# Top-k attention with an ELU feed-forward: the nine transposes of a step issued together, and their copies moved ahead of a mask

## The chip, the cores and the metric

The kernel runs on one core of one Trainium2 chip. The metric is the device time of one execution in microseconds (us), lower is better. Engines are named as in the profile: PE is TensorE (PEld its weight loads), DVE is VectorE, ACT is ScalarE, POOL is GpSimd, SP is SyncE.

## What is computed

Attention over 8 batches, 8 heads, 576 positions and 64 elements a head, in which each query row keeps only its 32 largest scores, and then a feed-forward over the 4608 rows that come out (512 to 2048 to 512), with an ELU between. The two weights are float64, so the kernel reads them as pairs of 32-bit words and makes float32 of them on the chip.

```python
scores = scale * np.matmul(q, k.transpose(0, 1, 3, 2))
kth = np.partition(scores, -32, axis=-1)[..., -32:-31]
scores = np.where(scores >= kth, scores, -1e9)
attn = np.exp(scores - np.max(scores, axis=-1, keepdims=True))
attn = attn / (np.sum(attn, axis=-1, keepdims=True) + 1e-09)
out = np.matmul(attn, v)
# (B, H, S, D) -> x of (B*S, H*D)
h = x @ w_in
g = np.where(h > 0.0, h, np.exp(np.minimum(h, 0.0)) - 1.0)
y = g @ w_out
```

## The kernel before, in words

**Steps.** The work is cut into 144 steps: 8 batches of 18. A step is a tile of 128 queries of one batch and a pair of heads, so it has two "rows" of scores, each 128 partitions by 576 keys. Of each batch 64 queries are left over; for them a step takes four heads, so that 128 partitions are full. Steps come in groups of two query tiles that share one attention product (in batch 0, and for the left-over queries, of a single tile).

**The loop** (L702) works on four steps at once. In iteration n it does, in this order of issue:

- scores of step n+2 (`scores`, L331), into two PSUM tiles `wide[0]` and `wide[1]` of two banks each, evicted by ScalarE into the tile `sc` (L339);
- the attention product of a group that is complete (`attend`, L470): 10 matmuls, each recorded twice in the profile, so that a run on two tiles shows 20; its result is copied by L497;
- the selection of step n on VectorE in four passes (`select`, L373, L378, L385): the 32 largest of each row, eight at a time;
- the mask of step n-1, one row ahead of the second pass and the other ahead of the third (`mask`): GpSimd takes a difference (L406), ScalarE makes the mask (L407) and the exponential with its sum (L408), in place in `sc`;
- the transposes of step n-2 (`turn`, L444, each a matmul with the identity) and their copies to the tile `et` on ScalarE (L445);
- the normalisation of step n-1 on GpSimd (`normalise`, L418 to L423 for the reciprocal of the sum, L425 for the two rows).

A step's `sc` is 128 by 1152, that is nine chunks of 128 columns. `turn` is called for three parts of them: `main` (chunks 0 to 3, all in the first row), `rest` (chunk 4, whose second half is in the second row) and `other` (chunks 5 to 8, in the second row). `main` and `other` each take a buffer of `ps_t`, a PSUM pool of two buffers that `attend` uses too. `rest` takes 128 columns beside the scores in the second bank of `wide[1]`, so the next scores wait for its copy.

**What is fed between.** Once a block of one to three tiles has all its heads, its feed-forward is cut into pieces: `hidden` (L545, w_in; two evictions by L555 and L558, an exponential by L560, minus one by L564 or inside the closing addition, which runs on GpSimd, L515, or VectorE, L517) and `project` (L573, w_out; evicted by L582, stored by SyncE, L585). They share a PSUM pool of two buffers. `feed` is called four times an iteration and issues as many pieces as the steps left and the work left ask for. In an iteration the pieces of the third feed stand between `rest` and `other`, those of the fourth between `other` and the next scores.

**Order.** From step 8 on the instructions of PE, ACT, DVE and POOL stand exactly in the order in which the code issues them; each engine takes its own in that order. The first eight steps are ordered by a scheduler and, beside their attention, hold the conversion of the weights. SyncE's transfers are not ordered by hand.

**Buffers that matter here.** `sc` has five buffers, `et` two, `ps_t` two. The tile `kqT`, with keys and queries transposed, has five; from batch 1 on VectorE fills it (L285), in the same order as its selections.

Of the kernel before, what the change touches and what calls it, by code (L numbers as in the profile page):

```python
# [24 lines left out]
class Tile:  # L25
# [6 lines left out]
    def __init__(self, b, qt, rows, block, cols):  # L32
        self.b, self.qt, self.rem = b, qt, qt == 4
        self.rows = rows
        self.block = block
        self.cols = cols
        self.ql = cols.stop - cols.start
# [21 lines left out]
class Step:  # L59
# [7 lines left out]
    def __init__(self, t, hp, group, at):  # L67
        self.t, self.hp = t, hp
        self.group, self.at = group, at
        self.masked = self.normal = self.turned = False  # L70
        if t.rem:
            rows = [(4 * hp, 0), (4 * hp + 2, 0), (4 * hp + 3, 1), (4 * hp + 1, 1)]
            self.heads = [
                (h, i, slice(64 * (n % 2), 64 * (n % 2) + 64))
                for n, (h, i) in enumerate(rows)
            ]
        else:
            self.heads = [(2 * hp + i, i, slice(0, 128)) for i in range(2)]
# [3 lines left out]
def kernel(  # L82
# [13 lines left out]
    J = S // P  # L96
# [216 lines left out]
    def turn_qk(whole=False):  # L313
        while turning:
            if next(turning[0], turning) is turning:
                turning.pop(0)
            elif not whole:
                return
# [3 lines left out]
    def scores(u):  # L322

        u.sc = scpool.tile([P, 2, S], FP32, tag="sc", name="sc")
        q0 = (QUERIES if u.t.b == 0 else S) + u.t.qt * P
        for half in range(2):
            for h, i, rows in u.heads:
                kq = kqT[u.t.b, h // 2]
                part = slice(i * D, (i + 1) * D)
                k0 = (KEYS if i == 0 and u.t.b == 0 else 0) + half * HS  # L330
                nc.tensor.matmul(  # L331
                    wide[i][rows, half, 0:HS],
                    kq[part, q0 : q0 + u.t.ql],
                    kq[part, k0 : k0 + HS],
                    start=True,
                    stop=True,
                )
        for i in range(2):
            nc.scalar.activation(  # L339
                u.sc[:, i, :].rearrange("p (a s) -> p a s", a=2),  # L340
                wide[i][:, :, 0:HS], AF.Copy, scale=scale,
            )

    def select_row(u, i, decoding):
        if i == 0:
            u.first = small.tile([P, 2, 8], FP32, tag="m1", name="m1")
            u.last = small.tile([P, 2, 8], FP32, tag="m4", name="m4")
        sc = u.sc[:, i, :]
        m = u.first[:, i, :]
        nc.vector.max(m, sc)  # L350
        wk = wkpool.tile([P, S], FP32, tag=f"wk{i}", name="wk")
        cur = sc
        for r in range(TOP_K // 8 - 1):
            nc.vector.match_replace(wk[:], m, cur, TAKEN)
            cur = wk[:]
            if r < TOP_K // 8 - 2:
                m = small.tile([P, 8], FP32, tag=f"m{i}", name="m")[:]
            else:
                m = u.last[:, i, :]
            nc.vector.max(m, cur)  # L360
            if r > 0 and decoding:
                hook()
            if r != 1:
                yield
# [64 lines left out]
    def turn(u, chunks):  # L429

        if u.turned:
            return
        g = u.group
        if g.et is None:
            g.et = etpool.tile([P, 2 * J + 1, len(g.tiles), P], FP32, tag="et", name="et")
        if chunks.stop - chunks.start == 1:
            ps = wide[1][:, 1, HS : HS + P]
        else:
            ps = ps_t.tile([P, JP], FP32, tag="t", name="eps")
        sc = u.sc[:, :, :].rearrange("p i s -> p (i s)")  # L440
        n = chunks.stop - chunks.start
        for c in range(n):
            c0 = (chunks.start + c) * P
            nc.tensor.transpose(ps[:, c * P : (c + 1) * P], sc[:, c0 : c0 + P], ident[:])  # L444
        nc.scalar.copy(  # L445
            g.et[:, chunks, u.at, :],
            ps[:, 0 : n * P].rearrange("p (c q) -> p c q", c=n),
        )
        if chunks.stop == 2 * J + 1:
            u.turned = True  # L450
            if u.at == len(g.tiles) - 1:
                closing.append(g)

    def attend(g):
        t = g.tiles[0]
        ps = ps_t.tile([P, JP], FP32, tag="t", name="avps")
        n = P if t.rem else sum(x.ql for x in g.tiles)
        for k in range(2 if t.rem else 1):
            hp = 2 * g.hp + k if t.rem else g.hp
            vt = vT[t.b, hp]  # L460
            for c in range(J + 1):
                for i in range(2):
                    chunk = J if c == J else i * (J + 1) + c
                    w = g.et[:, chunk, :, :].rearrange("p a q -> p (a q)")
                    cols = slice(0, n)
                    if t.rem:
                        c0 = R * (k if i == 0 else 1 - k)
                        w = w[:, c0 : c0 + R]
                        cols = slice(k * R, (k + 1) * R)
                    nc.tensor.matmul(  # L470
                        ps[i * D : (i + 1) * D, cols],
                        vt[:, 2 * J + i if c == J else i * J + c, :],
                        w,
                        start=(c == 0),
                        stop=(c == J),
                    )
        if t.rem:
            finish(t.block, 2, slice(2 * g.hp, 2 * g.hp + 2), t.cols,
                   ps[:, 0:n].rearrange("p (a q) -> p a q", a=2))
            return  # L480
        c0 = 0
        tiles = list(g.tiles)
        while tiles:
            blk, lo, parts = tiles[0].block, tiles[0].cols.start, 0
            while tiles and tiles[0].block is blk:
                parts += 1
                hi = tiles.pop(0).cols.stop
            finish(blk, parts, g.hp, slice(lo, hi), ps[:, c0 : c0 + hi - lo])
            c0 += hi - lo
# [112 lines left out]
    for b in range(B):  # L602
# [28 lines left out]
        for qts in order:  # L631
# [3 lines left out]
            for qt in qts:  # L635
                n = len(steps)
# [60 lines left out]
    def step(n):  # L697
        return steps[n] if 0 <= n < NS else None

    closing = []  # L700
    main, rest, other = slice(0, J), slice(J, J + 1), slice(J + 1, 2 * J + 1)
    for n in range(NS + 3):  # L702
        for fn, args in todo.pop(n, []):
            fn(*args)
        ahead, cur, prev, done = step(n + 2), step(n), step(n - 1), step(n - 2)
        if n < tight:
            turn_qk(True)
            if n < 3:
                scores(ahead)
            if n > 1:  # L710
                scores(step(n + 3))
            for i in range(2):
                passes = select_row(cur, i, n < tight - 1)
                next(passes)
                if i == 0:
                    while closing:
                        attend(closing.pop(0))
                elif prev:
                    normalise(prev)
                    turn(prev, main)  # L720
                    turn(prev, rest)
                    turn(prev, other)
                feed(n, 0.25)
                next(passes)
                mask(cur, i, True)
                feed(n, 0.25)
            continue
        if n == tight:
            ctx.enter_context(tc.manual_schedule(engines=engines))
        passes = select(cur) if cur else iter(range(4))  # L730
        if ahead and n > tight:
            scores(ahead)
        while closing:
            attend(closing.pop(0))
        next(passes)
        feed(n, 0.25)
        if prev:
            mask(prev, 0)
        turn_qk()
        next(passes)  # L740
        feed(n, 0.25)
        if done:
            turn(done, main)
            turn(done, rest)
        if prev:
            mask(prev, 1)
        next(passes)
        feed(n, 0.25)
        if done:
            turn(done, other)  # L750
        next(passes)
        if prev:
            normalise(prev)
        feed(n, 0.25)
        turn_qk(True)
# [36 lines left out]
```

## Time and profile before

| what | value |
|---|---|
| runs, median (lowest to highest) | 1643.64 us (1641.84 to 1643.79) |
| profiled execution, its own time | 1642.57 us |
| its span, first to last instruction | 1640.8 us |
| mean granted TensorE clock over the span | 0.974 |
| ACT: COPY of L445, 128x512, mean of 288 | 571 ns |
| ACT: COPY of L445, 128x128, mean of 144 | 269 ns |
| ACT: L407 and L408, mean of 288 each | 782 and 776 ns |
| POOL: L425, mean of 288 | 750 ns |
| DVE: MAX8 of L385, mean of 816 | 752 ns |
| PE: L444 into `ps_t`, mean of 1152 | 279 ns |
| PE: L470, mean of 2080 | 330 ns |

Matmuls are pipelined, so the mean of one is longer than the distance from one start to the next; distances between starts tell what a matmul costs on TensorE. A wait in the profile is idle time of an engine just before an instruction, put down to what released it. Where PEld waits but PE does not, the wait was partly covered by matmuls still running.

### The profile page before, as it was taken

To read this page: it belongs to the slowest core of one execution; us is meant where nothing else is said; L and a number is where in the kernel's file an instruction comes from. 1 tells how busy PE (TensorE), PEld (TensorE's weight loads), DVE (VectorE), ACT (ScalarE), POOL (GpSimd) and SP (SyncE) were. 2 spreads that over 40 slices of the span, in tenths; PEclk is the share of its full clock that TensorE was granted. 3 is DMA by queue.
4 is the path that set the end of the run, shared out by engine and by line. 5 is a ranking of instruction groups with operands and counts; after the bars stand their busy time and mean duration, and the time that the engine had idled before them with its cause. 6 is when DMAs were issued, how large, how long until landed. Compare 5 with 4: busy or idle time off the path is not lost.

```text
span 1640.8 us, 25344 instructions
## 1 busy us (share of the span) xinstructions
PE 1581.7 (96%) x8276; PEld 1011.8 (62%) x8276; DVE 1453.4 (89%) x2981; ACT 1187.7 (72%) x2400; POOL 708.7 (43%) x1534
## 2 busy tenths in 40 slices
PE   4788999999999999999999999999999999999999
PEld 3566777666575757555566666655557575755564
DVE  6987999999999999999999699999999599998000
ACT  6887778778695867778678686868759595958521
POOL 4775445445353534445335353535435353534300
PEclk8579999999999999999999999999999999999999
DMA  7431221012100310012100211012100201000000
GB/s 226 151 128 25 50 40 26 7 22 45 42 1 7 59 42 8 7 22 44 36 14 15 43 30 28 1 28 44 36 14 0 43 1 35 1 13 2 7 13 14
DMA packets 188037, 56.18 MB, mean 34 GB/s; under 512 B 178177, under 2 KB 179201, under 8 KB 187905
## 3 DMA queue, kind: packets, MB, share of 16 engines
q1 hardware_dynamic: 186704, 54.26, 14.1%
q8 instruction: 66, 1.08, 0.3%
q14 instruction: 67, 0.54, 0.1%
q10 hardware_dynamic: 1200, 0.30, 0.1%
HBM read 45.09 MB, written 9.44 MB: 33 GB/s over the span
## 4 chain that ended last, share of the span: by engine, by line
PE 76%; ACT 12%; DVE 7%; POOL 3%; issue 1%; DMA 1%; SPq 0%; ACTq 0%; DVEq 0%; POOLq 0%
PE ops L573 29%; PE hps L545 23%; PE avps L470 10%; PE scps L331 7%; PE eps L444 6%; DVE wk L378 3%; DVE m L385 3%; ACT sc L408 2%; ACT et L445 2%; ACT sc L407 2%; DVE m L373 1%; ACT n L564 1%; ACT n L555 1%; ACT sc L339 1%; ACT n L560 1%
## 5 line engine op out<-in xcount | busy, mean ns | idle before, releaser
L385 DVE MAX8 m<-wk 128x8 f32<-128x576 f32 x816 | 577.9, 752 | 0.3 <-POOL den L406 0.3
L545 PE MATMUL hps<-xT,w_in 128*128 128x256 f32 (+2 forms) x2432 | 545.8, 374 | 0.0
L573 PE MATMUL ops<-w_out,gT 128*128 128x512 f32 x1152 | 523.6, 599 | 0.0
L545 PEld LDWEIGHTS hps<-xT,w_in 128*128 128x128 f32 x2432 | 406.0, 192 | 100.1 <-issue 26.3
L378 DVE MATCH_REPLACE8 wk<-m,wk 128x576 f32<-128x576 f32 x544 | 401.4, 748 | 0.0
L573 PEld LDWEIGHTS ops<-w_out,gT 128*128 128x128 f32 x1152 | 209.0, 190 | 233.9 <-issue 232.8
L418 POOL TENSOR_SCALAR dene<-den 128x2 f32<-128x2 f32 x144 | 32.9, 228 | 686.5 <-ACT sc L408 686.1
L408 ACT ACTIVATE sc<-sc,den 128x576 f32<-128x576 f32 x288 | 223.6, 776 | 65.5 <-POOL den L406 44.2
L407 ACT ACTIVATE sc<-sc,m 128x576 f32<-128x576 f32 x288 | 225.3, 782 | 10.8 <-DVE m L385 10.7
L470 PE MATMUL avps<-et,vT 128*64 128x256 f32 (+2 forms) x2080 | 207.2, 330 | 17.4 <-ACT et L445 17.2
L425 POOL TENSOR_SCALAR sc<-sc,rec 128x576 f32<-128x576 f32 x288 | 213.0, 750 | 15.0 <-POOL rec L423 0.2
L331 PE MATMUL scps<-kqT 64*128 64x288 f32 (+1 forms) x1280 | 206.0, 442 | 13.6 <-ACT kqT L307 9.1
L339 ACT ACTIVATE sc<-scps 128x576 f32<-128x576 f32 x288 | 171.8, 647 | 65.1 <-PE scps L331 65.1
L445 ACT COPY et<-eps 128x512 f32<-128x512 f32 x288 | 164.6, 571 | 73.4 <-PE eps L444 73.4
L378 DVE MATCH_REPLACE8 wk<-m,sc 128x576 f32<-128x576 f32 x272 | 200.6, 748 | 0.0
L373 DVE MAX8 m<-sc 128x8 f32<-128x576 f32 x272 | 191.6, 749 | 8.8 <-ACT sc L339 8.8
L444 PEld LDWEIGHTS eps<-ident,sc 128*128 128x128 f32 x1152 | 144.9, 144 | 87.2 <-issue 52.7
L444 PE MATMUL eps<-ident,sc 128*128 128x128 f32 x1152 | 177.1, 279 | 13.7 <-POOL sc L425 13.7
L470 PEld LDWEIGHTS avps<-et,vT 128*64 128x64 f32 x2080 | 128.5, 142 | 98.8 <-ACT et L445 31.7
L515 POOL TENSOR_TENSOR gT<-n,gT 128x512 f32<-128x512 f32 (+1 forms) x119 | 164.9, 1386 | 31.2 <-ACT n L564 31.1
L331 PEld LDWEIGHTS scps<-kqT 64*128 64x128 f32 (+1 forms) x1280 | 111.3, 182 | 89.5 <-issue 43.8
L555 ACT ACTIVATE n<-hps 128x512 f32<-128x512 f32 (+1 forms) x156 | 87.3, 559 | 56.8 <-PE hps L545 56.0
(53 smaller groups left out, 1089.6 us busy)
## 6 DMA issues: line engine op xcount, KB each, us to landing
raw<-in_moe_w_in_dram SPq DMA_DIRECT2D x16, 512.0 KB, 6.1
vT<-in_v_dram SPq DMA_DIRECT2D x64, 128.0 KB, 2.5
raw<-in_moe_w_out_dram SPq DMA_DIRECT2D x16, 512.0 KB, 3.6
out_dram<-osb SPq DMA_DIRECT2D x32, 256.0 KB, 2.1
kin<-in_k_dram SPq DMA_DIRECT2D x112, 72.0 KB, 2.5
qin<-in_q_dram SPq DMA_DIRECT2D x112, 72.0 KB, 2.6
kin<-in_k_dram SPq DMA_DIRECT2D x8, 128.0 KB, 4.5
vT<-in_v_dram SPq DMA_DIRECT2D x64, 16.0 KB, 2.2
```

The source lines that it names most:

```text
L331: nc.tensor.matmul(wide[i][rows, half, 0:HS], kq[part, q0 : q0 + u.t.ql], kq[part, k0 : k0 + HS], start=True, stop=True,)
L373: nc.vector.max(found[i], cur[i])
L378: nc.vector.match_replace(wk[i], found[i], cur[i], TAKEN)
L385: nc.vector.max(found[i], cur[i])
L407: nc.scalar.activation(sc, sc, AF.Prelu, scale=-1.0, bias=low, alpha=1.0 / STEEP)
L408: nc.scalar.activation(sc, sc, AF.Exp, scale=-STEEP, bias=gap, accum_out=u.den[:, i : i + 1])
L425: nc.gpsimd.tensor_scalar(u.sc[:, i, :], u.sc[:, i, :], rec[:, i : i + 1], 1.0, ALU.mult, ALU.mult)
L444: nc.tensor.transpose(ps[:, c * P : (c + 1) * P], sc[:, c0 : c0 + P], ident[:])
L445: nc.scalar.copy(g.et[:, chunks, u.at, :], ps[:, 0 : n * P].rearrange("p (c q) -> p c q", c=n),)
L470: nc.tensor.matmul(ps[i * D : (i + 1) * D, cols], vt[:, 2 * J + i if c == J else i * J + c, :], w, start=(c == 0), stop=(c == J),)
L545: nc.tensor.matmul(blk.h[:, f % bank, :], w_in[:, i, f * P : (f + 1) * P], blk.xT[:, i, 0:n_tok], start=(i == 0), stop=(i == NC - 1),)
L573: nc.tensor.matmul(blk.o[:], blk.gT[f // NG][:, f % NG, s * P : (s + 1) * P], w_out[:, f, :], start=(f == 0), stop=(f == NF - 1),)
```

## The change

The four transposes of `other` are issued right after those of `main`, and `rest` after both, all ahead of the second row's mask and of the third feed. On ScalarE the two large copies and the small one then stand in one row ahead of the second row's L407 and L408; before, the copy of `other` stood behind that mask and behind the evictions of the third feed's pieces. A counter of chunks that are still to be turned takes the place of the test for the last chunk, since `other` is no longer the last call. The first eight steps keep their order of calls.

```diff
@@ class Step
         self.masked = self.normal = self.turned = False
+        self.left = 9
@@ turn
-        if chunks.stop == 2 * J + 1:
+        u.left -= n
+        if u.left == 0:
             u.turned = True
             if u.at == len(g.tiles) - 1:
                 closing.append(g)
@@ the loop
         if done:
             turn(done, main)
+            turn(done, other)
             turn(done, rest)
         if prev:
             mask(prev, 1)
         next(passes)
         feed(n, 0.25)
-        if done:
-            turn(done, other)
         next(passes)
```

## The prediction

> **What bounds the kernel now.** First the page: busy shares and the slices.
>
> ```profile
> PE 1581.7 (96%) x8276; PEld 1011.8 (62%) x8276; DVE 1453.4 (89%) x2981; ACT 1187.7 (72%) x2400; POOL 708.7 (43%) x1534
> ...
> PE   4788999999999999999999999999999999999999
> ...
> DVE  6987999999999999999999699999999599998000
> ```
>
> TensorE and VectorE are both full from the fifth slice on, so busy time alone doesn't say which sets the pace. I settled it with the timeline, step by step: the lag between the end of a step's last MAX8 (L385) and the start of that step's transposes (L444) two iterations later. It shrinks from 25.3 us (step 9) to 7.1 us (step 25, 317 us): there TensorE catches up and VectorE sets the pace. Then it grows: 10.5 us at 340, 13 at 500 to 600, 18 at 715, 30 at 915. So VectorE runs ahead and **TensorE sets the pace from about 340 us to the end**. The waits view says how VectorE's lead ends: its L285 transposes are held by the scores matmuls, once 14.2 us (before 931 us), once 16.9 us (before 1310 us). From 800 to 930 us the steps repeat at 11.53 and 9.22 us by TensorE's own work.
>
> ```profile
> DVE kqT L285 <- PE scps L331: 32.3, 3, 16.9
> PEld avps L470 <- ACT et L445: 31.7, 40, 3.8
> ...
> PE avps L470 <- ACT et L445: 17.2, 21, 3.3
> ...
> PE eps L444 <- POOL sc L425: 13.7, 5, 4.3
> ```
>
> (Columns: total us, times, longest.) The second and third lines are the wait that the change touches: the attention matmuls wait for the copy of the last four transposes. The fourth is where a later mask would show: transposes that wait for normalised rows. The timeline of one such step:
>
> ```profile
> 1487.09 0.60 PE L444 MATMUL eps<-ident,sc 128*128 128x128 f32 x4
> ...
> 1487.52 0.27 PE L444 MATMUL scps<-ident,sc 128*128 128x128 f32 x1
> ...
> 1489.67 0.57 ACT L445 COPY et<-eps 128x512 f32<-128x512 f32 x1
> ...
> 1490.13 0.27 ACT L445 COPY et<-scps 128x128 f32<-128x128 f32 x1
> 1490.21 0.60 PE L444 MATMUL eps<-ident,sc 128*128 128x128 f32 x4
> ...
> 1490.29 0.79 ACT L407 ACTIVATE sc<-sc,m 128x576 f32<-128x576 f32 x1
> ...
> 1491.92 0.65 PE L470 MATMUL avps<-et,vT 128*64 128x256 f32 x2
> ...
> 1492.68 0.59 ACT L445 COPY et<-eps 128x512 f32<-128x512 f32 x1
> ...
> 1493.32 2.37 PE L470 MATMUL avps<-et,vT 128*64 128x256 f32 x18 [0.76 <-ACT et L445]
> ```
>
> The last copy stands behind the second row's mask (L407, L408) and a block's evictions; 18 of the 20 attention matmuls wait for it. From 1491.92 to the next matmul (L545 at 1495.62) is 3.70 us; unhindered runs take 2.31.
>
> **The change, part by part.**
>
> (a) *The last copy no longer stands behind the mask.* I took every run of L470 after 300 us from its first matmul to the next other matmul. 24 of 55 runs on two tiles take 2.31 us, so that is the work. The excess of the others that start after 340 us adds up to 21.6 us, and one run of the remainder tiles has 0.93: **22.5 us**, 14.6 of it before 900 us. In the changed order the copy is issued 0.46 us after the main one (two L445 copies follow each other at that distance: 1489.67, 1490.13), and all three end before the scores matmuls do. All 22.5 go. What is late next is the remaining copy's release of the scores bank, (d).
>
> (b) *The run at 325 us.* Scores wait 2.46 us and attention 2.28 us there, at the end of VectorE's stretch. The second wait goes, the first grows by 0.46: **+1.8**.
>
> (c) *The single transpose comes after the four.* At 379, 540, 560, 767 and 1147 us it waited 0.51 to 0.77 us after the main four, for row two (L425's second half, 0.73 us behind the first) and for the scores' eviction (L339) from its bank. The four need row two as well, but not the bank: about 0.3 each, **+1.5**.
>
> (d) *Scores wait longer for their bank.* The single transpose's copy frees the bank that the next scores write; it now ends 0.46 us later, and the scores start when they did, since TensorE's work between is the same. Six steps are short of it already (at 379, 502, 560, 595, 684, 745 us): the full 0.46, 2.8 us. Eleven have 0.34 to 0.45 us of slack where they need 0.51: 1.1 us together. **-3.9**.
>
> (e) *The second row's mask starts 0.46 us later.* Queued behind it on ScalarE are the evictions of the fed blocks, and then L339; GpSimd's normalisation (L418 to L425) waits for it, and so do the next step's transposes. Slack of L425's end before those transposes: 1.1 to 8.7 us in nearly all steps after 340 us, typically 1.72 in the 9.22 us steps (1.44 for row two). Evictions have at least 1.5 us before their banks are needed again. So most of it is hidden. Without cover are the short steps of 7.5 us (at 379, 540, 560, 767, 1147 us), with 0.05 to 0.09 of slack: five times 0.46, **-2.3**.
>
> (f) *What VectorE doesn't let through.* Between 340 and 660 us the lag is small. A step's transposes can't start sooner after VectorE than the chain mask, copies, mask, normalisation takes: 6.2 us to the first normalised row in step 39 (450 us), where the first mask starts at once, and 6.7 with the added copy; about 9 to 10 where a block's evictions stand between the masks (5.5 us between them in step 51 in place of 2.3). At step 41 that leaves 2.0 us to gain, at step 51 3.4, at step 53 3.8, at step 59 5.8. The gains and losses above add up to 9.4 by step 59 (663 us); walked through these ceilings 5.4 are left: **-4.0**. Past that the lag grows faster than the gains, and both holds of VectorE (14.2 and 16.9 us) end with TensorE's scores, so they move with it.
>
> (g) *TensorE's work itself.* Starts are 0.109 us apart within the four, across to the single one, and from either to the next matmul; only towards scores is a step longer, 0.202 after transposes, and 0.093 is added after L545 or L573 instead. Regrouping moves that from one place to another: **0**. VectorE and GpSimd keep their order of instructions; on SyncE one q load changes places with an output store (landing 2.6 and 2.1 us, steps ahead of their use): 0, and 2.6 if that cover were gone. No transpose waits on its two-buffer pool: the bank that attention used is freed by L497, ahead of the masks on ScalarE; only at 410 us do transposes follow attention directly, 0.3 at most.
>
> Sum: 22.5 + 1.8 + 1.5 - 3.9 - 2.3 - 4.0 = **15.6 us**. The profiled execution took 1642.57 us (span 1640.8); 1642.57 - 15.6 = **1627.0**. The median of the runs shown is 1643.64, 0.07% above that execution.
>
> Two pages speak against it. By the Trainium skill, "Perfetto Trace Analysis", Identifying the Most-Contended Engine, matmul busy time is a poor measure and weight loading's busy share is to be used: 62% here, so VectorE (89%) would be the bound, and the time would stay near 1642.6. The lag in this trace says otherwise after 340 us. "TensorE: Matmul & The Clock Gate", Part 4, gives about 275 ns for a transpose in a kernel and says that transposes don't count as activity for the clock; nine in a row would be 2.5 us by it, against 0.98 by the trace's 0.109 us, and the mask would be late by some 1.1 us, still less than the usual slack. The granted clock of so long a run no row shows.
>
> **The rivals.**
>
> *All of it gets through.* VectorE's ceilings in (f) don't bind, since ScalarE's waits move too: 19.6 us, 1623.0; without (d) and (e) as well, 25.8 and 1616.8. For it: ceilings rest on single steps. Against: lags of 9 to 13 us up to 600 us.
>
> *VectorE is the bound up to 900 us.* It is busy 200.00 of 200.00 us in each window from 300 to 900 us. Then only later waits count: 7.9 (a), less about 1 for (d) and (e): 6.9 us, 1635.7. Against: the lag grows by 20 us in that stretch.
>
> *The wait is only renamed.* ScalarE reaches the main copy up to 5.4 us after its transposes (step 25); were it so late everywhere, attention would wait as before: 1642.6. Against: typical 0.3 to 3.1 us.
>
> *Slower: the mask's delay exceeds the slack.* The place is L407 of row two, behind a copy that waits for four more transposes. If one wait held all three copies for all nine transposes it would be 0.9 us late, still inside. It decides from 1.44 us (the slack of the single transpose in 9.22 us steps); some 58 steps then lose 0.58 us per 0.01 us, so 15.6 us are eaten at 1.7. At 2.0 us: 32 lost, 1659. For it: every step passes there. Against: no row shows such a wait.
>
> **How the numbers follow.** Forecast (gain 9 to 21 us) 0.60; all through 0.14; VectorE's bound 0.13; renamed 0.06; slower 0.07. Range: 1618.5 takes in all-through with smaller losses, 1637.0 the VectorE case with (d) and (e) doubled; 0.85 or so lies inside. A measurement of this kernel can tell some 0.2% (3.3 us) from no change: faster 0.87, same 0.06, slower 0.07.
>
> **What would show it.** Right: the waits of L470 for L445 are gone, runs of L470 take 2.31 us; L331's waits for L445 have grown to a few us; the first mask-to-mask distance is 0.46 us longer; steps at 800 to 930 us still repeat at 9.22 and 11.53; VectorE's two holds at L285 are shorter or equal, and the stretch from 1530 us to the end is 1.5 us shorter. Wrong: L444 waits for L425 in the 9.22 us steps (the mask's delay matters), or L470's waits are gone and the step times are longer (the clock, or transposes waiting for buffers), or the lag at 600 us is below 7 us and stays there (VectorE's bound).

## The result, and the profile after

The changed kernel takes **1631.73 us** (median of 6 runs, 1630.5 to 1633.75) where the kernel before takes 1643.25 (6 runs, 1641.61 to 1644.53): a ratio of 0.9933, 95% interval [0.992, 0.9945], 11.5 us or 0.7% less. The forecast was 15.6 us less, 1627.0. The profiled execution took 1631.07 us, span 1629.3, mean granted TensorE clock 0.977 (before 0.974).

The code stands one line lower than before after line 70 and two lower after line 449: L331 is now L332, L406 to L408 are L407 to L409, L425 is L426, L444 and L445 are L445 and L446, L470 is L472.

First the page of the changed kernel: busy time of the engines, and the slices of PE and DVE.

```profile
PE 1573.0 (97%) x8276; PEld 1005.0 (62%) x8276; DVE 1451.7 (89%) x2981; ACT 1185.9 (73%) x2400; POOL 710.6 (44%) x1534
...
PE   4788999999999999999999999999999999999999
...
DVE  6988999999999999999999799999999699999000
```

Next to nothing is to be seen in these lines: shares within a point, the same full slices. The waits view (total us, times, longest) shows what happened. Of the kernel before, the scores' wait for the copies, which stands beside the lines shown ahead of the change:

```profile
PEld scps L331 <- ACT et L445: 4.7, 8, 2.2
...
PE scps L331 <- ACT et L445: 1.7, 1, 1.7
```

And of the changed kernel:

```profile
PEld eps L445 <- POOL sc L426: 29.5, 34, 3.7
...
DVE kqT L286 <- PE scps L332: 25.7, 3, 16.3
...
PEld scps L332 <- ACT et L446: 19.1, 25, 3.1
PE eps L445 <- POOL sc L426: 17.9, 12, 3.4
...
PE scps L332 <- ACT et L446: 8.8, 9, 2.7
...
PEld avps L472 <- ACT et L446: 5.1, 4, 3.7
PE avps L472 <- ACT et L446: 3.8, 2, 3.3
```

The attention's wait for the copies has gone from 31.7 to 5.1 us on PEld (17.2 to 3.8 on PE), and what is left of it lies ahead of 340 us. The scores' wait for the same copies, which before was 4.7 on PEld and 1.7 on PE, is now 19.1 and 8.8, and the transposes wait a little more for GpSimd. The wait was taken away at one place, and a good half of it came back at another. The timeline of the step that was shown before makes the first half plain:

```profile
1477.98 1.04 PE L445 MATMUL eps<-ident,sc 128*128 128x128 f32 x8
...
1478.85 0.27 PE L445 MATMUL scps<-ident,sc 128*128 128x128 f32 x1
...
1480.57 1.06 ACT L446 COPY et<-eps 128x512 f32<-128x512 f32 x2
...
1481.51 0.28 ACT L446 COPY et<-scps 128x128 f32<-128x128 f32 x1
...
1483.01 2.38 PE L472 MATMUL avps<-et,vT 128*64 128x256 f32 x20
```

Eight transposes and the single one follow each other, the copies stand in one row, and the attention product runs through in 2.31 us from its first matmul to the next other matmul (1485.32), where it took 3.70.

**A ledger.** To compare kernels I add up, from step 27 (340 us) to the end, what each kind of run on TensorE takes beyond its unhindered time: attention beyond 2.31 us, scores beyond 1.17 us (first matmul of the run to the first of the next; the steps of left-over queries go by their own least times), and the transposes' waits, ahead of the nine and between them. The sums are of figures that aren't rounded. Each line is of one profiled execution, the time beside it the median of the runs.

| us after 340 us | attention | scores | transposes | sum | time (median) |
|---|---|---|---|---|---|
| before | 22.6 | 3.1 | 3.6 | 29.4 | 1643.25 |
| after | 0.0 | 16.1 | 5.0 | 21.2 | 1631.73 |

29.4 - 21.2 = 8.2; by the trace, the lead of the changed kernel grows from 3.1 us at step 27 to 11.5 at the end, that is 8.4. The ledger accounts for the difference after 340 us. So the question is why the scores lost 13.0 us where the forecast had 3.9.

### The profile page after: what moved, and what is told of

The parts are those of the page before. It is cut to its first block, busy times and chain, and to the rows that moved or that the text cites. A ratio compares the mean times of both kernels' runs of the same rounds, so it can differ in the third digit from the quotient of the medians.

```text
span 1629.3 us, 25324 instructions
## 1 busy us (share of the span) xinstructions
PE 1573.0 (97%) x8276; PEld 1005.0 (62%) x8276; DVE 1451.7 (89%) x2981; ACT 1185.9 (73%) x2400; POOL 710.6 (44%) x1534
## 4 chain that ended last, share of the span: by engine, by line
PE 69%; DVE 15%; ACT 8%; POOL 5%; issue 2%; DMA 1%; SPq 0%; ACTq 0%; DVEq 0%; POOLq 0%
PE ops L575 26%; PE hps L547 21%; PE avps L472 8%; PE scps L332 7%; DVE wk L379 6%; PE eps L445 5%; DVE m L386 5%; DVE m L374 2%; ACT sc L409 2%; ACT et L446 2%; POOL sc L426 1%; ACT sc L408 1%; POOL rec L421 1%; DVE wk L355 1%; DVE m L361 1%
## 5 line engine op out<-in xcount | busy, mean ns | idle before, releaser
L386 DVE MAX8 m<-wk 128x8 f32<-128x576 f32 x816 | 685.3, 1015 | 1.1 <-POOL den L407 0.8
L379 DVE MATCH_REPLACE8 wk<-m,wk 128x576 f32<-128x576 f32 x544 | 472.4, 1010 | 0.0
L409 ACT ACTIVATE sc<-sc,den 128x576 f32<-128x576 f32 x288 | 224.0, 778 | 90.0 <-POOL den L407 69.3
L408 ACT ACTIVATE sc<-sc,m 128x576 f32<-128x576 f32 x288 | 227.1, 788 | 19.5 <-DVE m L386 19.4
L332 PE MATMUL scps<-kqT 64*128 64x288 f32 (+1 forms) x1280 | 215.8, 443 | 21.2 <-ACT kqT L308 9.3
L379 DVE MATCH_REPLACE8 wk<-m,sc 128x576 f32<-128x576 f32 x272 | 235.8, 1008 | 0.0
L374 DVE MAX8 m<-sc 128x8 f32<-128x576 f32 x272 | 227.0, 1009 | 6.1 <-ACT sc L340 6.1
L426 POOL TENSOR_SCALAR sc<-sc,rec 128x576 f32<-128x576 f32 x288 | 214.0, 754 | 14.9 <-POOL rec L424 0.2
L332 PEld LDWEIGHTS scps<-kqT 64*128 64x128 f32 (+1 forms) x1280 | 114.4, 182 | 123.6 <-issue 61.1
L472 PE MATMUL avps<-et,vT 128*64 128x256 f32 (+2 forms) x2080 | 186.1, 326 | 3.8 <-ACT et L446 3.8
L379 DVE MATCH_VALUE_LOAD wk<-m,wk 128x8 f32 x544 | 187.2, 344 | 0.0
L445 PEld LDWEIGHTS eps<-ident,sc 128*128 128x128 f32 x1152 | 136.6, 144 | 70.6 <-issue 33.1
L446 ACT COPY et<-eps 128x512 f32<-128x512 f32 x288 | 153.5, 582 | 34.6 <-PE eps L445 34.1
L445 PE MATMUL eps<-ident,sc 128*128 128x128 f32 x1152 | 158.3, 279 | 18.7 <-POOL sc L426 17.9
L517 POOL TENSOR_TENSOR gT<-n,gT 128x512 f32<-128x512 f32 (+1 forms) x119 | 165.3, 1389 | 17.9 <-ACT n L566 17.8
L472 PEld LDWEIGHTS avps<-et,vT 128*64 128x64 f32 x2080 | 118.9, 141 | 74.6 <-issue 24.8
```

The source lines that it names most:

```text
L332: nc.tensor.matmul(wide[i][rows, half, 0:HS], kq[part, q0 : q0 + u.t.ql], kq[part, k0 : k0 + HS], start=True, stop=True,)
L374: nc.vector.max(found[i], cur[i])
L379: nc.vector.match_replace(wk[i], found[i], cur[i], TAKEN)
L386: nc.vector.max(found[i], cur[i])
L408: nc.scalar.activation(sc, sc, AF.Prelu, scale=-1.0, bias=low, alpha=1.0 / STEEP)
L409: nc.scalar.activation(sc, sc, AF.Exp, scale=-STEEP, bias=gap, accum_out=u.den[:, i : i + 1])
```

## The experiments

Three theories stood at first. **A**: the copy of `other` ahead of `rest` and of the mask delays both by about 0.48 us, and the mask's delay returns through GpSimd's queue to ScalarE's next copies. **B**: VectorE's pace takes back what TensorE gains, as step (f) of the forecast had it. **C**: only the place of the `rest` copy counts, 0.48 us behind, which frees the scores' bank later.

What A means is best seen in one step of 9.22 us. The timeline before, and the same step after:

```profile
870.92 1.47 POOL L425 TENSOR_SCALAR sc<-sc,rec 128x576 f32<-128x576 f32 x2
...
873.38 0.60 PE L444 MATMUL eps<-ident,sc 128*128 128x128 f32 x4
...
873.59 0.19 POOL L406 TENSOR_TENSOR den<-m,m 128x1 f32<-128x1 f32 x1
...
873.81 0.78 ACT L408 ACTIVATE sc<-sc,den 128x576 f32<-128x576 f32 x1 [0.58 <-POOL den L406]
...
876.74 0.57 ACT L445 COPY et<-eps 128x512 f32<-128x512 f32 x1
...
877.20 0.27 ACT L445 COPY et<-scps 128x128 f32<-128x128 f32 x1
...
877.91 1.24 PE L331 MATMUL scps<-kqT 64*128 64x288 f32 x8
```

```profile
863.73 1.48 POOL L426 TENSOR_SCALAR sc<-sc,rec 128x576 f32<-128x576 f32 x2
...
865.70 1.04 PE L445 MATMUL eps<-ident,sc 128*128 128x128 f32 x8
...
866.43 0.19 POOL L407 TENSOR_TENSOR den<-m,m 128x1 f32<-128x1 f32 x1
...
866.65 0.78 ACT L409 ACTIVATE sc<-sc,den 128x576 f32<-128x576 f32 x1 [1.09 <-POOL den L407]
...
869.58 1.06 ACT L446 COPY et<-eps 128x512 f32<-128x512 f32 x2
...
870.23 1.86 PE L332 MATMUL scps<-kqT 64*128 64x288 f32 x8
...
870.52 0.28 ACT L446 COPY et<-scps 128x128 f32<-128x128 f32 x1
...
870.86 0.78 PEld L332 LDWEIGHTS scps<-kqT 64*128 64x128 f32 x6 [0.33 <-ACT et L446]
```

Measure from the step's first transpose (873.38 before, 865.70 after). The normalisation of two rows starts 2.46 us ahead of it before and 1.97 after: it is 0.49 later, since the second row's mask was. Behind it on GpSimd stand half of a block's addition (L515, now L517, 1.3 us) and then the mask difference of the next step: 0.21 us after the first transpose before, 0.73 after. ScalarE's exponential waits for that difference, 1.09 us in place of 0.58. So ScalarE's whole row is late, and the main copy starts 3.88 us after the transposes in place of 3.36. On top of that, the `rest` copy stands one more copy behind. It ends 5.10 us after the first transpose in place of 4.09: 1.01 later, of which 0.52 is this round trip and 0.49 the place in the row. The scores, which were ready at the same moment, take 1.86 us in place of 1.24.

**1. `rest` copied first, `other` still ahead of the mask.** This takes away the place in the row and leaves the mask's delay.

```diff
             turn(done, main)
-            turn(done, other)
             turn(done, rest)
+            turn(done, other)
         if prev:
             mask(prev, 1)
```

> Order main, rest, other, all ahead of the second row's mask: the scores' bank is freed 0.48 us sooner than in the changed kernel, the mask starts as late as there. Theory A (two delays, the bank's and the mask's; the mask's comes a second time through GpSimd, where the next mask's difference L406 stands behind the late normalisation): the scores' waits after 340 us fall from 16 to about 8 us, those of the normal steps (870, 954, 1038 us and so on, 0.62 to 0.65 each) to about 0.15, transposes still wait for the normalisation as in the changed kernel; 3 to 6 us faster than it, 1626 to 1629. Theory C (only the bank's release counts): scores' waits fall to the 3 us of the kernel before, 1620. Theory B (VectorE's pace doesn't let TensorE gain more): 1631 to 1632 as in the changed kernel, with a wait of the same size elsewhere.

Measured: 1625.77 us (1623.47 to 1626.37), ratio 0.9894 [0.9878, 0.9909]. The scores' excess falls from 16.1 to 8.6 us; the waits of 0.6 us in the repeating steps after 760 us shrink to 0.1, since the slack there covers one of the two delays and not both. It speaks against B, which left no room for a gain, and against C, since 5.5 us of the 13.0 stay although `rest` is again where it was.

**2. `other` copied right behind the mask, still ahead of the feed.**

```diff
             turn(done, main)
-            turn(done, other)
             turn(done, rest)
         if prev:
             mask(prev, 1)
+        if done:
+            turn(done, other)
         next(passes)
         feed(n, 0.25)
```

> The four transposes of other stand behind the second row's mask, but ahead of the third feed: the copy waits for the mask and no longer for the feed's evictions; neither the mask nor the bank is later than in the kernel before. Theory A: waits of scores and of the transposes as in the kernel before (3 us and its few), attention's waits not gone but about 10 of 22.5 us left, since the mask's 1.75 us still stand ahead of the copy (0.9 where nothing is fed, 0.4 to 0.5 in the odd steps): 1629 to 1632, much like the changed kernel by another road. Theory C: the same. Theory B: the same time too, but with attention's waits near zero.

Measured: 1633.11 us (1630.22 to 1634.5), ratio 0.9939 [0.9925, 0.9953], within the interval of the change itself. Scores and transposes are as before (3.8 and 4.0 us), but 12.6 us of the attention's wait stay. So of the 22.6 us, 10.0 come from the evictions of the feed standing ahead of the copy, and 12.6 from the mask.

**3. By turn.** Only the last step of a group has the attention product behind it. In the others `other` goes behind the mask; in the last one it goes ahead of it, behind `rest`.

```diff
+        last = done and done.at == len(done.group.tiles) - 1
         if done:
             turn(done, main)
-            turn(done, other)
             turn(done, rest)
+            if last:
+                turn(done, other)
         if prev:
             mask(prev, 1)
+        if done and not last:
+            turn(done, other)
         next(passes)
```

> Main and rest first; other ahead of the mask only in a group's last step, where attention follows, and behind the mask in the others. Theory A: attention's waits near zero, the transposes' waits in the short steps back to those of the kernel before, scores' waits 3 to 5 us (no ripple through GpSimd into the step that precedes attention): 1621 to 1625. Theory C: about 1620, as e1. Theory B: 1630 to 1632.

Measured: 1623.88 us (1621.8 to 1624.37), ratio 0.9882 [0.9867, 0.9898]. No attention wait is left, and the scores' 8.2 us all lie before 745 us; of the waits of 0.6 us after it none is left, since in every other step nothing is delayed.

**4. The mask difference ahead of the normalisation.** If the round trip goes through GpSimd's queue, then the difference (L407), let past the normalisation, must not be late any more. From step 60 on, the first row's difference is issued first (called the hoist below):

```diff
...
-        else:
+        elif i == 1 or not u.gap:
             nc.gpsimd.tensor_tensor(gap, low, top, ALU.subtract)
...
         next(passes)
+        if cur and n >= 60:
+            cur.gap = True
+            cur.den = small.tile([P, 4], FP32, tag="den", name="den")
+            nc.gpsimd.tensor_tensor(
+                cur.den[:, 2:3], cur.last[:, 0, 7:8], cur.first[:, 0, 0:1], ALU.subtract
+            )
         if prev:
             normalise(prev)
```

> The changed kernel, but from step 60 on GpSimd takes the difference for a step's first mask (L406) ahead of the normalisation of the step before in place of behind it. Theory A: the second passage of the mask's delay is gone: scores' waits after 700 us of 0.62 to 0.65 fall to about 0.1, some 4 us less in all, 1627 to 1629. If the delay does not pass through GpSimd (only the copy's own 0.48 counts), the waits stay at 0.6 and the time at 1631 to 1632.

Measured: 1628.9 us (1625.43 to 1629.48), ratio 0.9911 [0.9894, 0.9927]. The time alone doesn't tell it from the change as it is; the ledger does. Of the seven waits of 0.47 to 0.65 us after 760 us six are gone and one is down to 0.2; with two of 0.2 that stay, 4.65 us become 0.57. At 660 us the scores' wait falls from 1.42 to 0.50, but there the transposes now wait 1.69: the difference waited for VectorE and held the normalisation behind it. This was the first sign of VectorE since the result.

**5. All of it behind the mask but the main copy.** This measures the price of `rest`: what if its copy comes last?

```diff
             turn(done, main)
+        if prev:
+            mask(prev, 1)
+        if done:
             turn(done, other)
             turn(done, rest)
-        if prev:
-            mask(prev, 1)
         next(passes)
```

> Nine transposes close together on TensorE, but on ScalarE the mask stands right behind the main copy, and the copies of other and rest behind the mask: the mask starts 0.25 us sooner than in the kernel before, and the copy that frees the scores' bank ends some 2.2 us later. Theory A (scores wait for that copy): the slack of the kernel before (1.46 us in every second step, 3.12 at best) no longer covers it; added waits of scores up to 83 us if every step pays on its own, 50 at least, attention's 22 saved: 1670 to 1700, slower than the kernel before. If the bank were not what scores wait for, the mask being early and the copies in time for attention, 1620 to 1625. Theory B (VectorE's pace): 1631 to 1650.

Measured: 1699.23 us (1697.67 to 1700.5), ratio 1.0342 [1.0328, 1.0357]. The scores' excess is 71.5 us, the largest in this study; the waits view of this kernel:

```profile
PEld scps L332 <- ACT et L446: 67.3, 80, 2.5
...
PE scps L332 <- ACT et L446: 31.3, 27, 2.0
```

The `rest` copy is the one on which the order of ScalarE hangs in every step; the copy of `other` counts only where the attention product follows, which is mostly every second step.

**6 and 7. VectorE's work cut.** Before and after, each with the last replacement round of the selection left out from step 8 on, so that 24 scores of a row are kept instead of 32. VectorE then has 1088 us of work in place of 1452 and runs far ahead of TensorE (from step 20 on the lag is never below 19.6 us in the first of the two); the other engines' work is the same.

```diff
-                nc.vector.match_replace(wk[i], found[i], cur[i], TAKEN)
+                if r < TOP_K // 8 - 2:
+                    nc.vector.match_replace(wk[i], found[i], cur[i], TAKEN)
...
-                nc.vector.max(found[i], cur[i])
+                if r < TOP_K // 8 - 2:
+                    nc.vector.max(found[i], cur[i])
```

> The kernel before, with the last of the three replacement rounds left out on VectorE from step 8 on, so it keeps the 24 largest scores: VectorE needs some 6.7 us a step in place of 9.6 and sets the pace nowhere after 200 us. TensorE no longer waits in the stretch up to 340 us: 1625 to 1640; attention still waits for its copies, 20 to 30 us in all. To be compared with the next kernel.

> The changed kernel with the same round left out. If VectorE's pace takes a part of the gain up to 700 us (term f of the prediction), then without that pace the change brings more than its 11.5 us: 14 to 20 us less than e6, and the scores' waits at some 470, 480 and 660 us, where ScalarE waits for VectorE ahead of the copies, are gone. If it takes none, 9 to 12 us less than e6, and the waits stay.

Measured: 1638.06 us for before (1635.64 to 1639.56, ratio 0.997 [0.9959, 0.998]) and 1626.85 for after (1624.27 to 1628.76, ratio 0.9897 [0.9881, 0.9913]). The change is worth 11.2 us with the cut and 11.5 without. The scores' excess stays at 14.6 us; of the waits of 1.4 to 1.5 us at 470, 481, 561 and 661 us only that at 470 is gone, down to 0.2. So B doesn't explain what was lost in this order. (The kernel before gains 5 us by the cut, all of it ahead of 340 us.)

**8. By turn, with the single transpose last in the group's last step.** The matmuls of `main` and `other` are issued ahead of `rest`, while the copies keep the order main, rest, other:

```diff
...
+        last = done and done.at == len(done.group.tiles) - 1
         if done:
-            turn(done, main)
-            turn(done, other)
-            turn(done, rest)
+            if last:
+                turn(done, main, other, rest)
+            else:
+                turn(done, main)
+                turn(done, rest)
         if prev:
             mask(prev, 1)
+        if done and not last:
+            turn(done, other)
```

> As e3, but in a group's last step TensorE transposes main, other, rest, and ScalarE copies main, rest, other: the single transpose no longer waits 0.55 to 0.8 us for its bank in five short steps. Theory A: 1 to 2 us less than e3, 1622 to 1624, no more than a run can show; attention's and scores' waits as in e3. Theory B: as e3.

Measured: **1622.18 us** (1621.34 to 1623.94), ratio 0.9875 [0.9862, 0.9889]. The transposes' waits fall from 4.8 to 2.6 us against experiment 3, the scores' rise from 8.2 to 9.3. It is the fastest kernel that does the whole computation; from experiment 3 it can't be told apart.

**9. By turn, with VectorE's work cut.**

> The by-turn order with the last replacement round of the selection left out from step 8 on, so that it keeps each row's 24 largest scores instead of 32 (part of the computation is left out). The by-turn kernel still has 8.2 us of the scores' waits for their bank, all before 745 us. If VectorE's pace is behind them, they fall to 3 us or less here and the time is 1616 to 1620 us, 18 to 21 us less than the 1638.06 of the kernel before with the same cut. If the row of ScalarE and GpSimd is behind them, 6 to 9 us of them stay and the time is 1621 to 1625 us, 13 to 17 us less than 1638.06.

Measured: 1611.82 us (1609.62 to 1612.06), ratio 0.9803 [0.9789, 0.9816], 26.2 us less than before with the same cut, further than either theory said. The scores' excess falls from 8.2 to 4.2 us. So in this order VectorE's pace does take something: the by-turn order gains 19.6 us with the whole selection and 26.2 with the cut one. The expectation had left out the stretch ahead of 340 us, where the cut lets this order gain some 2 us more.

**10. After, with VectorE's work cut and the difference first from step 20 on.**

> The changed kernel with the same cut (24 largest kept, from step 8 on) and, from step 20 on, with the first row's mask difference on GpSimd issued ahead of the normalisation of the step before instead of behind it. Without that hoist the time was 1626.85 us and the excess of the scores' runs 14.6 us, with waits of 1.4 us at 479, 559 and 659 us. If GpSimd's passage makes the scores wait, the excess falls to 8 us or less, the waits of 0.6 us are gone, and the time is 1620 to 1624 us. If the copies' own time on ScalarE makes them wait, the excess stays at 12 us or more and the time is 1625 to 1628 us.

**11. After, again, on the same chip.**

> The changed kernel as it is, again, beside the two others on the same chip: 1630 to 1633 us, and an excess of the scores' runs of about 16 us, most of it in the same steps as in its first profile (1.4 us at 380, 470, 481, 561 and 661 us, 0.6 us at 954, 1038, 1248, 1332 and 1416 us). If those places are accidents of one execution, half of them or more are elsewhere.

Measured: 1616.43 us (1613.36 to 1616.54, ratio 0.983 [0.9817, 0.9844]) for experiment 10, 10.4 less than the same kernel without the hoist (experiment 7) and below what was expected, since 2.7 us of it come ahead of 340 us. The scores' excess is 5.1 in place of 14.6 us; the waits of 1.4 at 479, 559 and 659 us and of 0.6 after 760 us are gone or down to 0.4. The changed kernel again took 1631.75 us (1631.35 to 1632.21, ratio 0.9928 [0.9916, 0.9941]), with a scores' excess of 15.9 us in the same places to a microsecond: 1.4 at 381, 482, 562, 662 us, 0.6 at 954, 1039, 1249, 1332, 1417. These places are no accident of one execution.

**12. After, with the whole selection, the difference first from step 44 on.**

> The changed kernel with its whole selection, and from step 44 (510 us) on the first row's mask difference issued on GpSimd ahead of the normalisation of the step before. With the last replacement round left out, the same hoist took the scores' excess after 510 us from 9.7 to 4.4 us, with the transposes' waits after 510 us as they were (2.3 us). If VectorE's pace stands behind GpSimd's passage between 510 and 670 us, the difference now waits for VectorE and the normalisation behind it: the transposes' waits after 510 us grow to 5 us or more, and the time is 1626.5 to 1630 us. If VectorE doesn't count there, they stay at 3 us or less, and the time is 1624 to 1626.5 us.

Measured: 1629.65 us (1627.04 to 1631.87), ratio 0.9911 [0.9894, 0.9929]. After 510 us the scores' excess falls from 10.5 (experiment 11) to 3.4 us, and the transposes' waits ahead of the nine, which were 2.2 us there, grow to 5.0, with 1.92 at 562 us alone. Lines of the waits view of experiments 7, 10 and 12, in this order, show the exchange. The edits move the lines of the code: the copies are L448, L449 and L447 here, the hoisted difference is L759 and L757.

```profile
PEld scps L332 <- ACT et L448: 15.6, 25, 1.9
...
PE scps L332 <- ACT et L448: 5.3, 7, 1.4
```

```profile
POOL den L759 <- DVE m L389: 9.9, 2, 5.0
...
PEld scps L333 <- ACT et L449: 6.6, 13, 0.9
...
PE scps L333 <- ACT et L449: 1.0, 3, 0.5
```

```profile
POOL den L757 <- DVE m L387: 205.5, 51, 7.7
...
PE eps L446 <- POOL sc L427: 23.6, 14, 4.3
...
PEld scps L333 <- ACT et L447: 13.1, 16, 3.2
```

From experiment 7 to 10 the hoist alone takes most of the scores' wait away (5.3 us on PE become 1.0), and the hoisted difference hardly waits for VectorE (9.9 us). In experiment 12 with the whole selection it waits 205.5 us for VectorE, the normalisation behind it is late, and the transposes wait for that (17.9 us on PE in the changed kernel, 23.6 here).

The ledger of all of them, the cut ones in the lower part:

| us after 340 us | attention | scores | transposes | sum | time |
|---|---|---|---|---|---|
| 1 rest first | 0.2 | 8.6 | 6.8 | 15.7 | 1625.77 |
| 2 behind the mask | 12.6 | 3.8 | 4.0 | 20.5 | 1633.11 |
| 3 by turn | 0.0 | 8.2 | 4.8 | 13.0 | 1623.88 |
| 4 difference first, from 60 | 0.0 | 10.7 | 6.9 | 17.6 | 1628.9 |
| 5 rest last | 4.5 | 71.5 | 0.2 | 76.2 | 1699.23 |
| 8 by turn, single last | 0.0 | 9.3 | 2.6 | 11.9 | 1622.18 |
| 11 after, again | 0.0 | 15.9 | 4.9 | 20.8 | 1631.75 |
| 12 difference first, from 44 | 0.0 | 7.2 | 8.8 | 16.0 | 1629.65 |
| 6 before, cut | 22.6 | 3.1 | 3.6 | 29.4 | 1638.06 |
| 7 after, cut | 0.1 | 14.6 | 5.0 | 19.7 | 1626.85 |
| 9 by turn, cut | 0.0 | 4.2 | 4.1 | 8.3 | 1611.82 |
| 10 after, cut, difference first | 0.0 | 5.1 | 5.0 | 10.1 | 1616.43 |

The sums order the kernels nearly as the times do; experiments 2 and 12 lie 1 to 3 us off, experiment 5 some 9, since what happens ahead of 340 us isn't in them.

## Why the prediction was right, and where it was not

The direction, the mechanism of the gain and the range held; the size was 4 us too large, and two of its terms were wrong for a reason that the sum hides. That the total came so near owes something to luck: (d) cost 9.1 us more than forecast, the 4.0 us of (f) didn't come on top, and of the gain ahead of 340 us 1.0 us came out of the first eight steps, in which executions of the same code differ.

**(a) The attention's wait, 22.5 us: right.** All 22.6 us of it are gone, and every run on two tiles after 340 us takes 2.31 us but one of 2.36.

**(b) The run at 325 us, 1.8: right there, but not for the stretch.** The interval ahead of step 26 is 2.5 us shorter and the next 0.5 longer: 2.0. But at step 25, where VectorE sets the pace, the chain from VectorE to the transposes had grown by 1.4 us (lag 7.06 before, 8.49 after); the forecast had nothing for that, though its own step (f) knew of the chain. That leaves 0.6 us. The profiled execution is 3.1 us ahead at step 27, and the other 2.5 are VectorE's: its last MAX8 of step 25 ends at 307.63 us in place of 310.12. Of these, 1.0 came out of the first eight steps (0.2 in the second profile of the same kernel), a part that varies from one execution to the next. The other 1.5 VectorE gained between steps 9 and 16, 1.5 in the second profile too: two of its waits, at 162 and 192 us, are 1.0 us shorter together in both (5.74 and 1.12 us become 5.5 and 0.34). The forecast had nothing for that stretch. So about 2 us ahead of 340 us come with the change, close to the 1.8, but mostly by another road.

**(c) The single transpose, 1.5: nearly right.** The waits inside the nine fall from 3.4 to 2.3 us: 1.1.

**(d) The scores' wait for their bank, -3.9: wrong, -13.0.** This is the step that failed. It took the `rest` copy to end 0.46 us later and everything else to start when it did. In the repeating steps it ends 1.0 us later, since the row of ScalarE is itself late by the round trip through GpSimd. The 13.0 us have three parts.

After 760 us seven steps lose 0.47 to 0.65 us each and two 0.2, 4.65 us in all; the forecast allowed 0.06 to 0.17 for each of eleven steps. Experiment 4 gives all but 0.57 of it back, with VectorE's work as it is, so here the passage through GpSimd's queue is **shown**; experiment 1, without the place in the row, leaves 0.1 in each, so it takes both delays to outrun the slack.

The six places that the forecast named lose 3.9 us in place of 2.8. Three of them, 0.36 before, have 0.85: experiment 1 brings 0.36 back and experiment 10 leaves 0.85, so they are the place in the row alone, as the forecast had it. At steps 31 and 49 (380 and 561 us) the main copy starts where it did, 5.0 us after the transposes, and the wait grows by 0.7. At step 67 (742 us) the main copy is 0.53 later, as in the repeating steps, and the wait grows by 1.0.

At steps 40, 41 and 59 (470, 481 and 661 us), where this term had nothing and term (f) had put VectorE's pace, 4.4 us are lost. There the main copy starts 1.35 to 2.4 us later after the transposes than before (at step 41 4.76 in place of 3.36), and the `rest` copy ends 1.8 to 2.9 us later. Each of these places follows, within two iterations, an attention wait that is gone (1.88 us at 465 and 1.60 at 648 us in the kernel before), so it looks as if that wait came back here; this is inferred from the order in time, and no run isolates it. At 470 us VectorE's pace stands behind it, since the wait goes when VectorE's work is cut (experiment 7); at 481 and 661 us it doesn't.

**(e) The second row's mask, -2.3: right in size.** The waits ahead of the nine transposes grow by 2.5 us, at the five short steps that were named. But "most of it is hidden" was read from the slack of L425 alone. The slack of the transposes was there (1.72 us became 1.22), and what passed through the same queue behind the normalisation, the next step's mask difference, had none. The delay had two takers, and I looked at one.

**(f) VectorE's pace, -4.0: the place right, the cause mostly not.** At steps 40, 41 and 59, two of them named by the forecast, 4.4 us are lost, but 2.8 of them stay when VectorE's work is cut. Without a quarter of VectorE's work the change is worth the same in all (11.2 against 11.5 us). After 340 us, where the term belongs, the ledger gives 29.4 - 19.7 = 9.7 us in place of 8.2: VectorE took 1.5, nearly all of it the wait at 470 us. Behind GpSimd's passage VectorE's pace stands as a second limit, as far as was tried, only in a short stretch. From step 44 to step 60 (510 to 675 us), by the times of their transposes against the kernel before, the changed kernel gains 2.0 us, with the hoist alone (experiment 12) 1.5, with VectorE's work cut alone (experiment 7) 2.1, and with both (experiment 10) 4.2; ahead of step 44 the hoist alone was not run. From step 60 on VectorE doesn't count: the hoist raises the gain from 5.7 to 10.6 us with the whole selection, and from 6.3 to 10.9 with the cut one. In the time of experiment 12, 2 us below the changed kernel's, which the intervals don't separate from nothing, this can't be seen: its profiled execution was 4.9 us behind the changed kernel's at step 27, ahead of the place of the hoist, and gained 4.4 on it from step 44 on. In the by-turn order VectorE takes more, 4.7 us after 340 us by the ledger (experiment 9 against 3), all of it ahead of step 60. The forecast took two limits that stand in a row as two terms of a sum, one of them too small.

**(g) TensorE's work, 0: right.** The steps of 9.22 and 11.53 us at 800 to 930 us repeat those of the kernel before to 0.01 us where no wait falls in them.

With these, after 340 us: 22.6 - 13.0 - 2.5 + 1.1 = 8.2 us; the forecast had 22.5 + 1.5 - 3.9 - 2.3 - 4.0 = 13.8 there.

**The rivals.** "The wait is only renamed" had 0.06 and was half right in size: 13 of 22.6 us came back, but as the scores' wait for their bank and not as the attention's, which is gone. The case that it had named, a main copy some 5 us behind its transposes, is new at steps 40, 41 and 59 alone. "VectorE is the bound up to 900 us" would have left 6.9 us; the cut runs refute it for this order. "All of it gets through" priced the change without (d) to (f) at 25.8 us; experiment 9, with VectorE's work cut, gains 26.2, but in another order and with 2 us of it from ahead of 340 us, so this is no check of that price. "Slower" didn't come: the mask was 0.48 us late (2.27 to 2.75 from the first mask to the second), far from 1.44.

**What would show it.** VectorE's two holds (14.2 and 16.9 us) became 9.1 and 16.3 us, and the stretch from the step at 1530 us to the end is 1.4 us shorter (110.81 to 109.45). L331's waits grew by more than "a few us", and that was the sign.

**The two pages.** With VectorE's busy share cut from 89 to 66% the kernel before gains 0.3%, all of it ahead of 340 us, so after that VectorE isn't its bound. The rule of the Trainium skill in "Perfetto Trace Analysis", Identifying the Most-Contended Engine, is to judge TensorE by its share of peak FLOPs (MFU) and by the busy share of its weight loads. The second misleads here: that share is 62% while TensorE sets the pace. The first was not worked out. The nine transposes take 0.98 us from the first start to the next matmul (1477.98 to 1478.96), at a granted clock of 1.00 in that microsecond. The 275 ns that "TensorE: Matmul & The Clock Gate", Part 4, gives for one bf16 transpose in a kernel would make 2.5 us of nine, as an estimate. A single record of L445 has 279 ns here too, but the records overlap, and the starts are 0.109 us apart.

**What stays open.** How the 1.4 to 1.7 us of the six steps at 380, 470, 481, 561, 661 and 742 us divide between the place in the row, the round trip and VectorE no run gives for each; experiment 1 leaves 0.9 us of four of them (380, 481, 561 and 661), and experiment 10, where VectorE's pace is taken away too, at most 0.43 of the same four. Why the second profile's first eight steps are 0.8 us slower than the first's was not tried.

## What to carry to other kernels

When an instruction is put ahead of others on an engine that takes its work in order, follow the delay through every queue that it enters, not only to the one reader that you had in mind: here 0.48 us on ScalarE went through GpSimd's normalisation to the small instruction queued behind it, and came back to ScalarE as a second 0.5 us. Of several results of one engine, copy first the one that frees a resource in every step, and hasten the other only in the steps that need it: by turn, the same idea gains 20 us in place of 11.5. Limits in a row aren't terms of a sum: in the 165 us from step 44 to 60 taking away either of two brought next to nothing, taking away both 2 us. And before two kernels are compared by their total, look at where along the run the difference arises: 5 us in the first 27 steps hid what a change did behind them.

## What the runs showed of the hardware

The length of VectorE's records differs between executions of the same instructions, and not the pace. The group of MAX8, of the first and of the second profile of the changed kernel (busy us and mean ns after the bar):

```profile
L386 DVE MAX8 m<-wk 128x8 f32<-128x576 f32 x816 | 685.3, 1015 | 1.1 <-POOL den L407 0.8
```

```profile
L386 DVE MAX8 m<-wk 128x8 f32<-128x576 f32 x816 | 576.5, 748 | 1.0 <-POOL den L407 0.8
```

1015 and 748 ns, and yet one MAX8 follows the other of a pair after 0.67 us in both, and the next pair after 2.1 us; MATCH_REPLACE8 has 1010 ns in the first profile where the kernel before has 748. VectorE's busy time in the two pages was 1451.7 and 1453.4 us all the same. So a longer mean in such a group is no slower engine, and distances between starts are what to compare.
